# Loads moved to SyncE, and more turned attention blocks sent by way of device memory

## The chip, the cores and the metric

The kernel runs on one core of a Trainium2 chip. The metric is the device time of one execution in microseconds, median of several runs. The engines are named as in the profile: PE (TensorE), DVE (VectorE), ACT (ScalarE), POOL (GpSimd) and SP (SyncE, which here only issues DMAs).

## What is computed

An attention with a threshold, whose result is the input of an MLP:

```python
scores = scale * np.matmul(q, k.transpose(0, 1, 3, 2))        # q, k, v: (8, 8, 576, 64)
thresh = np.max(scores, axis=-1, keepdims=True) - tau
scores = np.where(scores >= thresh, scores, -1000000000.0)
scores = scores - np.max(scores, axis=-1, keepdims=True)
attn = np.exp(scores)
attn = attn / (np.sum(attn, axis=-1, keepdims=True) + 1e-09)
attn_out = np.matmul(attn, v)
x = attn_out.transpose(0, 2, 1, 3).reshape(4608, 512)
h = x @ w_in                                                   # (512, 2048)
r = np.maximum(h, 0.0)
out = (r * r) @ w_out                                          # (2048, 512)
```

Everything is float32.

## The kernel before

**Visits and steps.** The attention goes over pairs of heads. A *visit* is one pair of heads with its query blocks (four of 128 queries and one of the 64 left over), and a *step* `s` is one query block of a visit. The first eight visits (n=0 to 7) split the first four pairs in two; from n=8 on a visit is a whole pair. The step loop is written out by hand, and each engine executes its instructions in the order in which the program issues them.

In a step the score products go to PSUM on PE (`scores`, `scores_of_two`), DVE takes the maxima (`maxima`, L305), ACT the exponentials (`exponents`, L320), DVE applies the threshold and sums (`threshold`, L332 to L335), and POOL divides (`divide`, L340 and L342).

**Turning.** For the product with v, the weights `w` must be turned, so that keys lie on partitions, in the tile `wT`. Up to n=10 PE does it (`turn`). From n=11 on (`by_dma`) DVE turns blocks of 32 by 32 into one of two halves of the tile `turned` (`turn_blocks`, L427 to L437), and DMAs from SyncE put the blocks in their places in `wT` (`place_blocks`). Two query blocks of a visit share one half of `turned`, a *pair* of blocks: pair 0 is query blocks 0 and 1, pair 1 is blocks 2 and 3, and pair 2 holds the left-over block. There are two ways to place one:

- Direct: 16 DMAs of 72 KB from `turned` to `wT` (L453; for pair 2 they are L458 and L466).
- Through device memory: one DMA of 1152 KB writes the half to the device tensor `aside` (`set_aside`, L404), and four DMAs of 288 KB read it back into `wT` (L445). `turned` is free again after the first.

From n=12 on visits are *paired*: the left-over blocks of an even and an odd visit are treated as one step at the head of the even visit, so two visits take nine steps. Only pair 0 of odd visits goes through `aside` before the change; the function `aside_first` says so. Lists by step, filled at L955 to L990, say in which step a pair is placed (`place_at`), a load is asked for (`load_at`), and q or k is turned by DVE for use (`prep_at`).

**Mixing.** `mix` (L499) multiplies the turned weights by v some steps after the visit's last block: three steps for an odd visit, four for an even one. A step with a mix is called *valued* in the code. It reads `wT`, so a placing of the next blocks to the same rows has to wait for it.

**Loads.** From n=11 on, q, k, v and left-over rows are asked for some steps ahead and put in a queue `loads`. `some_loads` (L198), called four times in a step, takes one or two from it and issues them. Which engine issues them is decided in its last line: SyncE up to two steps after the first step of n=11 (`first_dma + 2`), GpSimd after that.

**The MLP.** As soon as 256 rows of x are complete, they are a *chunk*. Its products (`unit`, L658; `product`, L764) are cut into pieces that the function `fill` puts between the attention's instructions of each step, at a rate worked out in advance. The MLP uses sums of weight factors, made by GpSimd and in part by DVE (`factor_sum`, L589), and sums of tokens (L635).

**The order in a step.** Steps before n=12's first (`first_late`) are issued in the body of the last loop, later ones by `late_step`. In the body the blocks of n=11 are turned near the end of a step, after the threshold of the step (L1167). In `late_step` they are turned right behind the exponentials (`turn_last`).

Of the kernel before, what the change touches and what calls it, by code (L numbers as in the profile page):

```python
# [19 lines left out]
def kernel(  # L20
# [10 lines left out]
    nc = tc.nc  # L31
# [6 lines left out]
    NBLK = S // P  # L38
# [159 lines left out]
    def some_loads():  # L198
        for _ in range(min(1 + (len(loads) > 8), len(loads))):
            to, src = loads.popleft()  # L200
            (nc.gpsimd if state["step"] > first_dma + 2 else nc.sync).dma_start(out=to, in_=src)  # L201

    def arrived(t):
        assert all(x[0].tensor.name != t.tensor.name for x in loads)
# [109 lines left out]
    def exponents(vis, i):  # L314
        w, sc, st = weights[vis, i]
        mx, thr, bias = (st[:, j, 0:len(sc)] for j in range(3))
        nc.scalar.activation(out=bias, in_=mx, func=AF.Copy, scale=-SCALE)  # L317
        nc.scalar.activation(out=thr, in_=mx, func=AF.Identity, bias=ntau8)
        for u in range(len(sc)):
            nc.scalar.activation(out=w[:, u, :].rearrange("p (h k) -> p h k", h=2), in_=sc[u],  # L320
                                 func=AF.Exp, bias=bias[:, u:u + 1], scale=SCALE)
# [78 lines left out]
    def set_aside(vis, pair):  # L400

        t = aside[len(outside) % 4]
        at = list(blocks).index((vis, pair)) % 2 * NB
        nc.sync.dma_start(out=t, in_=turned[:, at:at + NB])  # L404
        outside[vis, pair] = t.rearrange("(b r) (j x) -> r j b x", r=32, j=4)
# [33 lines left out]
    def place_blocks(vis, pair, which=range(4)):  # L439

        wb = blocks[vis, pair]
        if (vis, pair) in outside:
            for j in range(4):
                g0 = (ONE, TWO)[pair] // REST
                nc.sync.dma_start(out=wT[j * 32:j * 32 + 32, g0:g0 + 4, :, :].rearrange("r b c q -> r b (c q)"),  # L445
                                  in_=outside[vis, pair][:, j, :, :])
            return
        for qb in which:
            rows = slice(qb * 32, qb * 32 + 32)
            for j in range(4):  # L450
                to = wT[j * 32:j * 32 + 32, :, :, :]
                if pair < NBLK // 2:
                    nc.sync.dma_start(out=to[:, (ONE, TWO)[pair] // REST + qb, :, :].rearrange("p c q -> p (c q)"),  # L453
                                      in_=wb[rows, :, j, :, :].rearrange("p c u q -> p (c u q)"))
                    continue
                at = slice(qb % 2 * 32, qb % 2 * 32 + 32)
                if paired(vis):
                    nc.sync.dma_start(out=to[:, (LEFT if qb < 2 else ODD) // REST, :, at], in_=wb[rows, j:2 * KB:4, :])  # L458
                else:


                    first = j if qb < 2 else KB + (j - KB) % 4
                    n = len(range(first, KB if qb < 2 else 2 * KB, 4))
                    c = first // 4
                    first += 2 if qb < 2 else -KB
                    nc.sync.dma_start(out=to[:, LEFT // REST, c:c + n, at], in_=wb[rows, first:first + 4 * n - 3:4, :])  # L466
# [151 lines left out]
    def some_later(engine):  # L618
        if later[engine]:
            make(*later[engine].popleft())  # L620
# [194 lines left out]
    def paired(n):  # L815

        return n >= 3 * HP
# [4 lines left out]
    steps = [(n, i) for n in range(len(visits)) for i in visits[n][1]]  # L822
    NST = len(steps)

    def by_dma(n):

        return n >= 3 * HP - 1

    first_dma = next(s for s in range(NST) if by_dma(steps[s][0]))
# [30 lines left out]
    state = {"us": 0.0, "left": 0.0, "step": 0, "free": False, "rounded": 0, "usable": 0, "then": [], "last": [], "made": 0}  # L860
# [76 lines left out]
    for s, (n, i) in enumerate(steps):  # L937
        if s < HP * FIRST:
            x = int(n > 0 and i == 0)
        else:  # L940
            x = 2 if (n, i) in ((2 * HP - 2, FIRST + 1), (2 * HP - 1, FIRST + 1), (2 * HP, FIRST)) else 1
# [14 lines left out]
    for s, (n, i) in enumerate(steps):  # L956
        if not by_dma(n) or i != visits[n][1][0] or paired(n) and n % 2:
            continue
        nxt = n + (2 if paired(n) else 1)
        more = nxt < len(visits)  # L960
        if paired(n):

            a, b = (1, 2) if paired(n - 1) else (2, 2)
            place_at[s + a].append((n, 2, (0, 1)))
            place_at[s + b].append((n, 2, (2, 3)))
            place_at[s + 3].append((n, 0))
            place_at[s + 5].append((n, 1))
            place_at[s + 8].append((n + 1, 0))
            place_at[s + 9].append((n + 1, 1))
            prep_at[s - 1].append(lambda n=n: prep_part(q, n))  # L970
            load_at[s - 1].append(lambda n=n: load_part(q, n + 1))
            load_at[s + 2].append(lambda n=n: load_v(n))
            prep_at[s + 3].append(lambda n=n: prep_part(q, n + 1))
            load_at[s + 4].append(lambda n=n: load_v(n + 1))
        else:
            place_at[s + 3].append((n, 0))
            place_at[s + 4].append((n, 1))
            place_at[s + 5].append((n, 2))
        if more:
            a, b, c, d = (s + 1, s + 5, s + 7, s + 8) if paired(n) else (s + 1, s + 2, s + 4, s + 4)  # L980
            load_at[a].append(lambda n=nxt: load_part(k, n))
            if paired(n):
                load_at[a].append(lambda n=nxt: load_left(n))
            prep_at[b].append(lambda n=nxt: prep_part(k, n))
            load_at[b].append(lambda n=nxt: load_part(k, n + 1))
            if not paired(n):
                load_at[s - 8].append(lambda n=nxt: load_left(n))
            load_at[b].append(lambda n=nxt: load_part(q, n))
            prep_at[c].append(prep_left)
            prep_at[d].append(lambda n=nxt: prep_part(k, n + 1))  # L990
# [16 lines left out]
    def turn_last(s):  # L1007
        if s <= NST:
            turn_blocks(*steps[s - 1])
            if aside_first(steps[s - 1][0]) and steps[s - 1][1] == 1:  # L1010
                set_aside(steps[s - 1][0], 0)

    def aside_first(n):

        return paired(n) and n % 2

    def at_least(count, made):
        while waiting and state["made"] < made + count:
# [2 lines left out]
    def late_step(s):  # L1021

        on = s < NST
        odd = on and steps[s][1] % 2 == 1
        if on:
            n, i = steps[s]
            if not odd:
                scores_of_two(s)
            after()
            maxima(s, [area(u, odd) for u in range(2)])  # L1030
            some_later("gpsimd")
            exponents(n, i)
        turn_last(s)
        valued = s in mixes and s < END

        def place():
            for what in place_at[s]:
                place_blocks(*what)

        if not valued:  # L1040
            place()

        def values():
            if s in mixes:
                while (visits[mixes[s][0]][0] // HP + 1) * S - RING > read_to["x"]:
                    piece()
                mix(*mixes[s])
                for j in chunk_at.get(s, ()):
                    add_chunk(j)

        if s == END:
            values()
        quarter = rate(s) / 4 if s < END else 1e9
        made = state["made"]
        fill(quarter)
        some_later("gpsimd")
        after()
        if on:
            threshold(n, i)
            for fn in prep_at[s] + load_at[s]:  # L1060
                fn()
            divide(n, i)
        some_later("vector")
        fill(quarter)
        after()
        some_later("gpsimd")
        if valued:
            at_least(1, made)
            made = state["made"]
            values()  # L1070
            place()
        some_loads()
        some_later("vector")
        some_loads()
        fill(quarter)
        some_loads()
        fill(quarter)
        some_loads()
        if valued:
            at_least(2, made)  # L1080

    for s in range(END + 1):
# [32 lines left out]
            turn(*old, 1)  # L1115
        if on:
            exponents(n, i)
            for p in now[1:]:
                round_weights(p, 0)
            if at == 1:  # L1120
                split_left(n)
            if lay:
                prep(n + 1)
            elif now:
                for p in now:
                    round_weights(p, 1)
# [36 lines left out]
        if smooth:  # L1163
            fill(quarter)
            after()
            some_later("gpsimd")
        if 0 < s <= NST and by_dma(steps[s - 1][0]):  # L1167
            m, x = steps[s - 1]
            turn_blocks(m, x)
        for what in place_at[s]:  # L1170
            place_blocks(*what)
        some_loads()
# [53 lines left out]
```

## Time and profile before

The time is 1391.8 us, median of 3 runs (1389.78 to 1392.49). The profiled execution has a span of 1391.4 us and a mean granted PE clock of 0.979.

| engine | busy us | share of the span | instructions |
|---|---|---|---|
| PE matmul | 1320.4 | 95% | 9112 |
| PE weight load | 1092.0 | 78% | 9112 |
| DVE | 940.3 | 68% | 2026 |
| ACT | 583.1 | 42% | 1357 |
| POOL | 987.8 | 71% | 1229 |

The chain of work that ended last lies on PE for 68% of the span and on POOL for 14%, with 6% on DVE. These are shares of one path through the program and not idle times: while the chain runs on POOL, PE may well be busy with work that came earlier.

The DMA issues that matter for the change, from issue to landing (median):

| issue | from | count | KB each | us |
|---|---|---|---|---|
| wT<-turned (direct) | SP | 608 | 72 | 2.1 |
| wT<-turned (pair 2) | SP | 192 | 36 | 2.0 |
| aside<-turned | SP | 12 | 1152 | 4.4 |
| wT<-aside | SP | 48 | 288 | 5.2 |
| ql<-in_q_dram | POOL | 96 | 72 | 3.1 |
| kl<-in_k_dram | POOL | 88 | 72 | 3.0 |
| vs<-in_v_dram | POOL | 48 and 48 | 128 and 32 | 3.2 and 2.3 |
| q_left<-in_q_dram | POOL | 88 | 8 | 2.0 |

How to read what follows: in the view of waits a line names the engine and line that waited, what released it, and then the time in total, how often and the longest. In a timeline a line has start, duration, engine, source line, operation and count, and in brackets the idle time before it with its releaser. `<-` reads "from". An instruction that only issues a DMA takes issue time on its engine; the transfer goes on by itself.

### The profile page before, as it was taken

How to read it: one execution, taken by the hardware profiler on the slowest of the kernel's cores; microseconds unless marked ns; L12 is line 12 of the kernel's file. 1: busy time of each engine (PE TensorE's matmuls, PEld its weight loads, DVE VectorE, ACT ScalarE, POOL GpSimd, SP SyncE). 2: the span in 40 equal slices, each digit the busy share in tenths (PEclk: the TensorE clock that was granted, in tenths of full speed). 3: DMA queues.
4: the chain of work that ended last, by engine and by line, in shares of the span. 5: the costliest groups of instructions: out<-in, count | busy, mean ns of one | idle time of the engine just before them, and what ended most of it. 6: DMA issues, size and time to landing. Idle time of an engine off the chain costs nothing.

```text
span 1391.4 us, 25676 instructions
## 1 busy us (share of the span) xinstructions
PE 1320.4 (95%) x9112; PEld 1092.0 (78%) x9112; DVE 940.3 (68%) x2026; ACT 583.1 (42%) x1357; POOL 987.8 (71%) x1229
## 2 busy tenths in 40 slices
PE   7899999979999899989999999999999899999998
PEld 5676567758887778778887879888887778889997
DVE  6877775867786777767777787777676757722231
ACT  4777664215353434435342435353524242512322
POOL 3679774778786959597878788879696856653451
PEclk8999999989999999999999999999999999999999
DMA  8755431434545454545435454545434443230000
GB/s 153 162 149 142 121 82 26 95 68 141 101 137 105 120 129 105 130 92 139 103 114 117 101 141 94 147 99 145 93 114 100 106 113 86 89 81 1 16 16 16
DMA packets 200976, 142.28 MB, mean 102 GB/s; under 512 B 157552, under 2 KB 161936, under 8 KB 199312
## 3 DMA queue, kind: packets, MB, share of 16 engines
q1 hardware_dynamic: 180256, 109.25, 32.7%
q0 software_dynamic: 18288, 31.11, 8.7%
q8 instruction: 72, 1.18, 0.4%
q10 hardware_dynamic: 2304, 0.29, 0.2%
q14 instruction: 56, 0.46, 0.1%
HBM read 64.75 MB, written 23.59 MB: 63 GB/s over the span
## 4 chain that ended last, share of the span: by engine, by line
PE 68%; POOL 14%; DVE 6%; issue 3%; ACT 3%; SPq 3%; DMA 2%; ACTq 0%; DVEq 0%; POOLq 0%
PE big L658 21%; PE big L764 21%; PE big L502 9%; PE big L284 6%; PE big L550 3%; PE big L268 3%; POOL w L342 3%; POOL g L589 2%; PE big L729 2%; SPq L453 2%; PE big L381 2%; DVE st L305 2%; DVE w L332 1%; POOL gsum L589 1%; POOL q_left L201 1%
## 5 line engine op out<-in xcount | busy, mean ns | idle before, releaser
L305 DVE TENSOR_REDUCE st<-big 128x1 f32<-128x576 f32 x288 | 204.4, 748 | 154.0 <-PE big L284 119.9
L342 POOL TENSOR_SCALAR w<-w,st 128x576 f32<-128x576 f32 x269 | 245.5, 922 | 23.7 <-DVE st L335 16.4
L764 PE MATMUL big<-wo,gsum 128*128 128x256 f32 x1088 | 245.1, 382 | 2.3 <-DVE gsum L784 2.3
L764 PEld LDWEIGHTS big<-wo,gsum 128*128 128x128 f32 x1088 | 204.9, 190 | 40.2 <-issue 9.5
L332 DVE SCALAR_TENSOR_TENSOR w<-big,st,w 128x576 f32<-128x576 f32 x269 | 207.0, 805 | 27.7 <-ACT w L320 27.6
L658 PE MATMUL big<-xT,w_in_sb 128*128 128x128 f32 x1536 | 188.1, 277 | 3.7 <-DVE osb L794 2.3
L658 PEld LDWEIGHTS big<-xT,w_in_sb 128*128 128x128 f32 x1536 | 180.7, 193 | 9.5 <-issue 3.8
L764 PE MATMUL big<-wo,g 128*128 128x256 f32 x816 | 186.6, 382 | 0.2
L502 PE MATMUL big<-wT,vs 128*64 128x128 f32 (+7 forms) x1700 | 171.8, 360 | 15.6 <-DMA wT<-turned 10.0
L320 ACT ACTIVATE w<-big,st 128x576 f32<-128x576 f32 x269 | 183.6, 733 | 0.0
L340 POOL TENSOR_SCALAR st<-st 128x2 f32<-128x2 f32 (+1 forms) x148 | 36.4, 246 | 197.6 <-DVE w L332 190.0
L764 PEld LDWEIGHTS big<-wo,g 128*128 128x128 f32 x816 | 151.2, 190 | 26.7 <-issue 7.5
L502 PEld LDWEIGHTS big<-wT,vs 128*64 128x64 f32 (+1 forms) x1700 | 97.7, 138 | 86.6 <-issue 34.0
L317 ACT ACTIVATE st<-st 128x2 f32<-128x2 f32 (+1 forms) x148 | 30.3, 205 | 293.9 <-DVE st L305 293.0
L670 DVE TENSOR_TENSOR g<-big,g 128x512 f32<-128x512 f32 x96 | 64.9, 676 | 99.5 <-PE big L658 94.0
L284 PE MATMUL big<-kT,qT 64*128 64x256 f32 (+3 forms) x768 | 110.6, 425 | 1.4 <-DVE w L332 1.4
L284 PEld LDWEIGHTS big<-kT,qT 64*128 64x128 f32 x768 | 86.7, 191 | 17.2 <-issue 9.0
L427 DVE STREAM_TRANSPOSE turned<-w 128x512 f32<-128x512 f32 x100 | 70.0, 700 | 32.4 <-POOL w L342 22.4
L540 POOL TENSOR_TENSOR gsum<-g 128x512 f32<-128x512 f32 x34 | 44.0, 1294 | 67.0 <-ACT g L667 63.5
L666 ACT ACTIVATE g<-g 128x512 f32<-128x512 f32 x96 | 60.3, 629 | 68.6 <-DVE g L670 68.6
L667 ACT ACTIVATE g<-g 128x512 f32<-128x512 f32 x128 | 80.7, 630 | 4.1
L658 PE MATMUL big<-t,g 128*128 128x128 f32 x512 | 67.2, 290 | 12.7 <-POOL g L589 10.8
(119 smaller groups left out, 2264.1 us busy)
## 6 DMA issues: line engine op xcount, KB each, us to landing
wT<-turned SPq DMA_DIRECT2D x608, 72.0 KB, 2.1
aside<-turned SPq DMA_DIRECT2D x12, 1152.0 KB, 4.4
wT<-aside SPq DMA_DIRECT2D x48, 288.0 KB, 5.2
wo<-in_moe_w_in_dram SPq DMA_DIRECT2D x16, 512.0 KB, 4.6
wo<-in_moe_w_out_dram SPq DMA_DIRECT2D x16, 512.0 KB, 3.7
out_dram<-osb POOLq DMA_DIRECT2D x32, 256.0 KB, 2.5
ql<-in_q_dram POOLq DMA_DIRECT2D x96, 72.0 KB, 3.1
wT<-turned SPq DMA_DIRECT2D x192, 36.0 KB, 2.0
```

The lines of the kernel that those rows point to most:

```text
L284: nc.tensor.matmul(big[to, at + x0:at + x1], lhsT, keys[u * D:(u + 1) * D, x0:x1], start=True, stop=True)
L305: nc.vector.tensor_reduce(out=mx[:, u:u + 1], in_=sc[u], axis=AX.XY, op=ALU.max)
L320: nc.scalar.activation(out=w[:, u, :].rearrange("p (h k) -> p h k", h=2), in_=sc[u], func=AF.Exp, bias=bias[:, u:u + 1], scale=SCALE)
L332: nc.vector.scalar_tensor_tensor(out=wu, in0=sc[u], scalar=thr[:, u:u + 1], in1=wu, op0=ALU.is_ge, op1=ALU.mult, accum_out=sm[:, u:u + 1])
L342: nc.gpsimd.tensor_scalar(out=w[:, u, :], in0=w[:, u, :], scalar1=z[:, u:u + 1], scalar2=rcp[:, u:u + 1], op0=ALU.add, op1=ALU.mult)
L427: move(wb[:, 0:h, :, :], whole_[:, 0, :, :, :])
L502: nc.tensor.matmul(ps[u * D:(u + 1) * D, :], vs[n % 2][rows, u * (NBLK + 1) + c, :], wT[rows, at // REST:(at + ps.shape[1]) // REST, NBLK ...
L658: nc.tensor.matmul(to[:, f, :], factor(j, p, q, c)[:, f * P:(f + 1) * P], part[:, c, :], start=(p in "125" and f == 0 and c == 0), stop=(p ...
L666: nc.scalar.activation(out=to, in_=to if src is None else src, func=AF.Relu)
L667: nc.scalar.activation(out=to, in_=to, func=AF.Square)
L670: nc.vector.tensor_tensor(out=x, in0=to, in1=x, op=ALU.add)
L764: nc.tensor.matmul(to, left[:, f, :], wo[:, slot, f, :], start=(f == 0), stop=(f == HF - 1))
```

## The change

There are three parts. All queued loads are issued by SyncE. Pair 0 and pair 1 of every visit from n=11 on go through `aside`, with the exception of pair 1 of odd paired visits, which is still placed directly; and a pair that goes out is placed later in its step, behind the first load. The blocks of n=11, the 12th visit, are turned behind the maxima and exponentials of the next step and no longer near its end, and its pair 0 is placed one step earlier. The purpose is to relieve GpSimd of issuing loads, to relieve SyncE of issuing sixteen DMAs for a pair, and to have the 12th visit's blocks ready sooner.

```diff
     def some_loads():
         for _ in range(min(1 + (len(loads) > 8), len(loads))):
             to, src = loads.popleft()
-            (nc.gpsimd if state["step"] > first_dma + 2 else nc.sync).dma_start(out=to, in_=src)
+            nc.sync.dma_start(out=to, in_=src)
...
-            place_at[s + 3].append((n, 0))
+            place_at[s + 2].append((n, 0))
             place_at[s + 4].append((n, 1))
             place_at[s + 5].append((n, 2))
...
     def turn_last(s):
         if s <= NST:
             turn_blocks(*steps[s - 1])
-            if aside_first(steps[s - 1][0]) and steps[s - 1][1] == 1:
-                set_aside(steps[s - 1][0], 0)
-
-    def aside_first(n):
-
-        return paired(n) and n % 2
+            n, i = steps[s - 1]
+            if i % 2 and by_dma(n) and goes_out(n, i // 2):
+                set_aside(n, i // 2)
+
+    def goes_out(n, pair):
+
+        return pair < NBLK // 2 and not (pair and paired(n) and n % 2)
...
         valued = s in mixes and s < END
 
-        def place():
-            for what in place_at[s]:
-                place_blocks(*what)
+        todo = list(place_at[s])
+
+        def place(all_):
+            for what in list(todo):
+                if all_ or not goes_out(*what[:2]):
+                    place_blocks(*what)
+                    todo.remove(what)
 
         if not valued:
-            place()
+            place(False)
...
             values()
-            place()
         some_loads()
+        place(True)
         some_later("vector")
...
         if on:
             exponents(n, i)
+            if s and by_dma(steps[s - 1][0]):
+                turn_last(s)
...
-        if 0 < s <= NST and by_dma(steps[s - 1][0]):
-            m, x = steps[s - 1]
-            turn_blocks(m, x)
         for what in place_at[s]:
             place_blocks(*what)
```

## The prediction

> **What bounds the kernel now.** I read the busy times first, then the stages, then the waits of TensorE, then GpSimd and SyncE where those waits fall. The stage view has, for each stretch, its length and each engine's busy time with its number of instructions, then the granted clock, DMA share and GB/s. The stretches are: all that lies before the 12th visit (n=11), that visit, the paired visits, the last chunks.
>
> ```profile
> 0.00:229.00 229.00, 205.49 (x1510) 143.09 (x1512) 163.10 (x361) 149.76 (x368) 158.50 (x189) 0.97 0.53 127
> 229.00:300.00 71.00, 61.02 (x339) 47.52 (x335) 48.23 (x98) 16.79 (x45) 50.96 (x60) 0.90 0.28 60
> 300.00:1216.00 916.00, 882.39 (x6134) 743.85 (x6133) 681.89 (x1502) 371.97 (x864) 708.04 (x917) 0.98 0.47 114
> 1216.00:1391.00 175.00, 171.48 (x1136) 157.59 (x1135) 47.04 (x67) 44.54 (x83) 70.25 (x64) 1.00 0.10 26
> ```
>
> TensorE (PE, first number after the length) is the bound everywhere, so only its idle time and its half-speed clock can be won. In the 12th visit it is idle 71.0 - 61.0 = 10.0 us; in the paired visits 916.0 - 882.4 = 33.6 us. The rest of its idle time lies before 229 us or after 1216 us, where the change touches nothing. Next, who ends those waits (us in total, times, longest):
>
> ```profile
> PE big L658 <- POOL g L589: 10.8, 8, 3.7
> PE big L658 <- POOL gsum L589: 10.1, 4, 3.8
> PE big L502 <- DMA wT<-turned: 10.0, 2, 6.2
> ```
>
> The third line is the whole idle time of the 12th visit: the value products of its mix (L502) wait for blocks that SyncE hasn't finished placing. The first two are 20.9 of the 33.6 us in the paired visits: products of the MLP wait for factor sums that GpSimd makes (L589). The other 12.7 us end on VectorE in pieces of about 1 us. Why GpSimd is late shows in its timeline ahead of the longest such wait:
>
> ```profile
> 597.78 2.69 POOL L201 DMA_DIRECT2D kl<-in_k_dram  x4
> 600.47 1.07 POOL L201 DMA_DIRECT2D q_left<-in_q_dram  x2
> 601.62 0.22 POOL L340 TENSOR_SCALAR st<-st 128x2 f32<-128x2 f32 x1
> 601.94 1.63 POOL L342 TENSOR_SCALAR w<-w,st 128x576 f32<-128x576 f32 x2
> 603.51 2.72 POOL L201 DMA_DIRECT2D q_left<-in_q_dram  x5
> ...
> 609.11 3.38 POOL L589 TENSOR_TENSOR g<-g,w_in_sb 128x512 f32<-128x512 f32 x2
> ```
>
> The reader is to see that 11 load issues (L201) of 2.69 + 1.07 + 2.72 = 6.48 us stand in GpSimd's queue between its last idle moment (591.5 us) and the sums that TensorE waits for. TensorE's own timeline has the price, in brackets:
>
> ```profile
> 610.88 0.49 PE L658 MATMUL big<-t,g 128*128 128x128 f32 x2 [3.69 <-POOL g L589]
> 612.55 6.50 PE L658 MATMUL big<-t,g 128*128 128x128 f32 x30 [1.18 <-POOL g L589]
> ```
>
> I went back from each of the larger GpSimd waits in this way: since GpSimd's last idle moment there were 3.4 to 12.0 us of L201, always more than the wait (2.65 us at 318, 1.13 at 384, 2.64 at 469, 1.03 at 544, 3.69 at 607, 2.00 at 1026, 3.81 at 1112).
>
> For the 12th visit, SyncE's timeline against TensorE's:
>
> ```profile
> 244.16 30.00 SPq L453 DMA_DIRECT2D wT<-turned  x32
> 274.26 10.40 SPq L466 DMA_DIRECT2D wT<-turned  x16
> ```
> ```profile
> 281.11 1.30 PE L502 MATMUL big<-wT,vs 128*64 128x320 f32 x2 [6.16 <-DMA wT<-turned]
> 286.23 7.08 PE L502 MATMUL big<-wT,vs 128*64 128x320 f32 x38 [3.83 <-DMA wT<-turned]
> ```
>
> SyncE needs 48 issues in a row; the second block pair is turned at 263 us, its 16 issues end at 274.3, the left-over ones at 284.7, and the mix, which TensorE reached at 275.0, is released near 286.
>
> [...] GpSimd pays in its own time: 368 issues of L201 occupy it for 66.9 + 64.6 + 59.1 + 48.2 = 238.8 us. [...] the trace has SyncE standing 50.6 us in 12 waits of the placing line L445 on `aside<-turned`. [...] the clock is 0.90 in the 12th visit and 0.97 or 0.98 exactly in the sub-stages with long waits, 1.00 at 800 to 1000 us, where there are nearly none.
>
> **The change part by part.**
>
> *Loads to SyncE.* GpSimd loses 238.8 us of 988 us. SyncE gains 184 q and k loads x 0.49 us (its rows at L179), 96 of v x 0.53 (L225), 88 of q_left x 0.43 (L196): 90 + 51 + 38 = 179 us.
>
> *Turned blocks through device memory.* By the program 38 block pairs are placed directly now (608 issues of 72 KB), 12 by way of `aside`. Afterwards 38 go out (2 per even visit, 1 per odd one, 2 of the 12th) and 12 stay direct. SyncE loses 26 x 16 = 416 issues x 0.589 = 245 us and gains 26 x 0.342 + 104 x 0.386 = 49 us. In sum SyncE's issue time goes 179 - 245 + 49 = -17 us: it has the room. Latency of a pair: direct 16 x 0.63 + 2.1 = 12 us; out and back 4.4 + 4 x 0.43 + 5.2 = 11.3 us, the same within 1 us, and even mixes have 10 us or more between the last placed packet and its use.
>
> *DMA engines.* 26 more writes of 1.18 MB as 128 packets of 9216 B at 359 ns make 1195 us of engine time, and loads as 128 B packets at 13.2 ns instead of packets of 4 KB at 246 ns cost some 590 us more; over 16 engines 112 us, so the share goes from 0.47 to about 0.59 in the paired visits. Hidden, as no transfer is bandwidth-bound.
>
> *Order on SyncE.* Placing a pair that goes out now waits for its `aside` (about 5 us) near the end of the step, and loads queue behind it. Steps take 8.6 us on average and a load is consumed 3 or 4 steps after it is queued, so I charge nothing for slips of 5 us. The sharp place is the direct pair of odd visits: its 16 issues end at 437.50 us, the last packet at 438.63, and the mix's second group reads it at 440.55; over the 12 odd mixes this slack is 1.4 to 6.7 us. The queue ahead of it (four issues after the even mix, four loads) is done about 4 us before its blocks are turned, so I charge 3 us in all for it.
>
> *12th visit turned behind the maxima.* The second pair is turned at about 256.5 instead of 263 us, as GpSimd's division (253.6) and the maxima (254.8) allow. Out at 256.9, landed at 261.5, four issues to 263.2. The 16 left-over issues then start at the turn of block 4 (265.2) and end at 275.5, landed at 277.5. TensorE arrives at 275.0: 2.5 us of wait remain of 10.0, saving 7.5.
>
> *Sum.* GpSimd's waits: 20.9 us, of which I take 85% (GpSimd also waits 190.0 us for the thresholds on VectorE, and part of its lead will end there): 18. The waits on VectorE, partly late through GpSimd (22.4 us of VectorE's turning waits are for its division): 4 of 12.7. Clock: the mean 0.979 over 1391 us means 29 us lost, of which 7 before 229 us and 7 in the 12th visit, so some 15 in the paired visits; 11 of these return with the waits. 12th visit: 7.5 + 2.5, since the mix in half clock took 7.08 us for 38 products where later mixes take 4.8 for 40. Together 18 + 4 + 11 + 10 = 43, less 3: **1391.8 - 40 = 1352 us**.
>
> **The rivals.**
>
> *Another wait takes over (A).* GpSimd gets ahead and then stands for VectorE's thresholds, so that its sums come hardly earlier. For it: those 190.0 us of waits, in 61 pieces. Against it: in each case above there was more load time than wait in one unbroken run of work. If half of the paired visits' gain goes: 1391.8 - 10 - 16 = 1366 us.
>
> *Loads weren't what mattered (B).* Only the 12th visit gains: 1391.8 - 10 = 1382 us. For it: GpSimd is busy only 71% of the span. Against it: the same unbroken runs.
>
> *SyncE becomes the bound (C).* One queue in order carries loads, write-outs, and placings with waits. If each odd mix, with as little as 1.4 us of slack, waits 5 us and drags 1.7 us of half clock behind it, that is 12 x 6.7 = 80 us against 40 won: 1432 us; at 4 us each, 1400 us. For it: SyncE then issues about 47 us and waits some 20 us in each 77 us of two visits. Against it: its issue time falls, and the direct pairs, the sharp ones, are still taken early in the step.
>
> **How the numbers follow.** Chances: forecast 0.60 (1338 to 1360), A 0.17, B 0.09, C 0.14, with 0.02 of C's ending within 0.2% of before. So faster 0.86, same 0.02, slower 0.12. The range is 1337 to 1386 us: the low end is all 33.6 us, 12 us of clock and 9 us of the visit; the high end takes in A and B and leaves C out.
>
> **What would show it.** L201 appears only under SyncE; GpSimd falls to about 750 us busy; the two L658 lines on GpSimd lose most of 20.9 us; the clock of the paired visits is 0.99 or 1.00; the mix of the 12th visit waits under 4 us. Wrong, if L502 shows waits on `wT<-turned` or `wT<-aside` at odd mixes, if VectorE's turning of q or k waits for loads, or if waits of L658 on GpSimd stay while L340's waits for VectorE grow by what the loads took.

## The result, and the profile after

The changed kernel takes 1367.0 us (median of 4 runs, 1365.4 to 1368.6) against 1392.1 us before: a ratio of 0.982 with a 95% interval of 0.980 to 0.984. That is 25 us less. The forecast was 40 us less, 1352 us, with a range of 1337 to 1386 us. Of all the runs below one was slow, at a lower granted clock (0.94, 1382.4 us, of the version with pair 0 placed directly), and is left out.

The stage view after, in the same stretches of time as before (length, busy PE, PEld, DVE, ACT, POOL with their counts, clock, DMA share, GB/s):

```profile
0.00:229.00 229.00, 205.40 (x1508) 142.97 (x1510) 163.23 (x362) 149.43 (x367) 158.16 (x189) 0.97 0.53 127
229.00:300.00 71.00, 66.30 (x392) 53.81 (x388) 55.01 (x120) 20.93 (x54) 44.31 (x46) 1.00 0.51 111
300.00:1216.00 916.00, 891.79 (x6245) 754.18 (x6244) 672.27 (x1492) 370.99 (x863) 500.58 (x579) 0.99 0.64 146
```

The first stretch is unchanged. In the second, TensorE's idle time went from 10.0 to 4.7 us and its clock from 0.90 to 1.00. In the third it went from 33.6 to 24.2 us (the stretch now holds some later work too), while GpSimd's busy time fell by 207 us and the DMA share rose from 0.47 to 0.64. Over the whole page GpSimd is busy 757.8 us instead of 987.8.

TensorE's waits after (total, times, longest):

```profile
PE big L658 <- POOL gsum L589: 14.0, 3, 5.5
...
PE big L658 <- ACT g L678: 4.4, 1, 4.4
...
PE big L502 <- DMA wT<-turned: 3.6, 1, 3.6
```

Eight waits on `g` of L589 are gone. But three waits on `gsum` of L589 are left and have become longer: 14.0 us in three instead of 10.1 us in four. The 4.4 us on ScalarE (L678) are a new wait, at 601 us: ScalarE stands there behind exponentials that wait 5.01 us for VectorE's maxima (L317 on L305). It is in the trace of every version below with the loads on SyncE and in none with the loads on GpSimd. This is the longest wait on `gsum`:

```profile
313.63 3.35 PE L658 MATMUL big<-xT,gsum 128*128 128x128 f32 x14 [5.52 <-POOL gsum L589]
```

GpSimd's own waits say what holds it now. Before:

```profile
POOL st L340 <- DVE w L332: 190.0, 61, 11.3
...
POOL osb L635 <- DMA out_dram<-osb: 1.0, 2, 0.5
```

After:

```profile
POOL st L340 <- DVE w L332: 344.5, 88, 11.5
...
POOL osb L635 <- DMA out_dram<-osb: 17.4, 9, 5.1
```

The first line is large and grew by 154.5 us: GpSimd waits for VectorE's thresholds when it has nothing else to do. The second is small, and the experiments below show that it is the one that matters. GpSimd's timeline ahead of that longest wait, of the changed kernel:

```profile
304.23 0.62 POOL L742 DMA_DIRECT2D out_dram<-osb  x1
304.87 1.30 POOL L589 TENSOR_TENSOR gsum<-w_in_sb,g 128x512 f32<-128x512 f32 x1
311.04 0.72 POOL L635 TENSOR_TENSOR osb<-xT,t 128x256 f32<-128x256 f32 x1 [4.87 <-DMA out_dram<-osb]
311.71 0.57 POOL L742 DMA_DIRECT2D out_dram<-osb  x1
312.30 1.27 POOL L589 TENSOR_TENSOR gsum<-w_in_sb,g 128x512 f32<-128x512 f32 x1
```

The token sum called T4 (L635) writes its result over rows of `osb` that GpSimd has just sent to the output (a *write-out*, L742). It must stand until that transfer has landed, and the factor sum behind it, the one TensorE waits for, stands with it. The same place in the kernel before:

```profile
313.47 0.61 POOL L742 DMA_DIRECT2D out_dram<-osb  x1
314.11 1.30 POOL L589 TENSOR_TENSOR gsum<-w_in_sb,g 128x512 f32<-128x512 f32 x1
315.33 2.15 POOL L201 DMA_DIRECT2D vs<-in_v_dram  x3
317.47 0.76 POOL L635 TENSOR_TENSOR osb<-xT,t 128x256 f32<-128x256 f32 x1
```

There the write-out landed 2.6 us after its issue, under three load issues that GpSimd had to make anyway. After the change the loads are gone from this place, and the write-out took 6.75 us. SyncE's timeline in that moment shows why it might:

```profile
301.66 1.73 SPq L445 DMA_DIRECT2D wT<-aside  x4
303.44 5.87 SPq L201 DMA_DIRECT2D vs<-in_v_dram  x7
```

Four reads of 288 KB and seven loads of v had just been issued on SyncE's queue. From the DMA packets in the trace: the first packet of this write-out began 4.77 us after its issue (1.16 us where nothing collides), and until it landed SyncE's queue kept the 16 engines busy for 100% of the time, with 331 packets of 2304 B and 2064 of 256 B. Averaged over the 33 write-outs that GpSimd issues, the landing went from 2.88 to 3.57 us, and those over 3.5 us from 5 to 12.

### The profile page after: what moved, and what is told of

The parts are those of the page before. It is cut to its first block, busy times and chain, and to the rows that moved or that the text cites. A ratio compares the mean times of both kernels' runs of the same rounds, so it can differ in the third digit from the quotient of the medians.

```text
span 1363.7 us, 25169 instructions
## 1 busy us (share of the span) xinstructions
PE 1307.4 (96%) x9112; PEld 1085.8 (80%) x9112; DVE 929.3 (68%) x2026; ACT 583.1 (43%) x1357; POOL 757.8 (56%) x861
## 3 DMA queue, kind: packets, MB, share of 16 engines
q1 hardware_dynamic: 327232, 162.07, 52.4%
q10 hardware_dynamic: 2304, 0.29, 0.2%
## 4 chain that ended last, share of the span: by engine, by line
PE 84%; DVE 4%; POOL 4%; ACT 3%; DMA 2%; issue 2%; SPq 1%; ACTq 0%; DVEq 0%; POOLq 0%
PE big L764 28%; PE big L658 26%; PE big L502 11%; PE big L284 8%; PE big L550 3%; PE big L268 3%; PE big L729 2%; PE big L381 2%; DVE st L305 1%; DVE w L332 1%; DMA out_dram<-osb 1%; ACT wT L382 1%; ACT w L320 1%; POOL w L342 1%; POOL g L589 1%
## 5 line engine op out<-in xcount | busy, mean ns | idle before, releaser
L305 DVE TENSOR_REDUCE st<-big 128x1 f32<-128x576 f32 x288 | 204.5, 749 | 151.9 <-PE big L284 116.8
L340 POOL TENSOR_SCALAR st<-st 128x2 f32<-128x2 f32 (+1 forms) x148 | 36.8, 248 | 349.8 <-DVE w L332 344.5
L658 PE MATMUL big<-xT,w_in_sb 128*128 128x128 f32 x1536 | 187.3, 277 | 2.2 <-DVE osb L794 2.1
L658 PEld LDWEIGHTS big<-xT,w_in_sb 128*128 128x128 f32 x1536 | 180.1, 193 | 7.5 <-issue 4.0
L502 PE MATMUL big<-wT,vs 128*64 128x128 f32 (+7 forms) x1700 | 168.8, 356 | 9.1 <-ACT wT L382 4.0
L502 PEld LDWEIGHTS big<-wT,vs 128*64 128x64 f32 (+1 forms) x1700 | 96.4, 136 | 78.4 <-issue 26.5
L317 ACT ACTIVATE st<-st 128x2 f32<-128x2 f32 (+1 forms) x148 | 30.3, 205 | 273.0 <-DVE st L305 272.0
L284 PE MATMUL big<-kT,qT 64*128 64x256 f32 (+3 forms) x768 | 107.8, 419 | 0.0
L658 PE MATMUL big<-xT,gsum 128*128 128x128 f32 x512 | 68.8, 290 | 14.5 <-POOL gsum L589 14.0
```

What stands on the lines that cost most here:

```text
L284: nc.tensor.matmul(big[to, at + x0:at + x1], lhsT, keys[u * D:(u + 1) * D, x0:x1], start=True, stop=True)
L305: nc.vector.tensor_reduce(out=mx[:, u:u + 1], in_=sc[u], axis=AX.XY, op=ALU.max)
L502: nc.tensor.matmul(ps[u * D:(u + 1) * D, :], vs[n % 2][rows, u * (NBLK + 1) + c, :], wT[rows, at // REST:(at + ps.shape[1]) // REST, NBLK ...
L658: nc.tensor.matmul(to[:, f, :], factor(j, p, q, c)[:, f * P:(f + 1) * P], part[:, c, :], start=(p in "125" and f == 0 and c == 0), stop=(p ...
```

## The experiments

Each is timed against runs of the kernel before on the same chip. Those took 1391.9 to 1393.2 us from chip to chip, so a difference between versions of different chips is good to about 1 us. Theory M in the expectations is: the extra waits come from write-outs that land late. The numbers below are medians of 4 runs, with pair 0 placed directly of 3, with more pairs through device memory alone of 12.

**Loads alone.** The kernel before with the one line:

```diff
-            (nc.gpsimd if state["step"] > first_dma + 2 else nc.sync).dma_start(out=to, in_=src)
+            nc.sync.dma_start(out=to, in_=src)
```

> The kernel before, with the loads issued by SyncE and nothing else changed. Theory M (what is left of the waits after the change comes from write-outs of osb that land late because the DMA engines are fuller): 1372 to 1378 us, most of the gain of the paired visits, with the 12th visit unchanged at about 10 us of TensorE idle time; write-outs issued by GpSimd land in 2.9 us on average as before (3.6 after the change), so GpSimd's token sum L635 waits under 6 us in all for them (17.4 after the change). Rival R (SyncE hasn't the room for loads as long as each pair costs 16 issues): 1385 us or more, with waits of L502 on wT<-turned at the odd mixes or of VectorE on loads.

Measured: 1362.6 us, ratio 0.979 (0.977 to 0.980). One part of the change alone gains 30.5 us, more than the whole change, and the time is 9 us below M's range. TensorE's waits:

```profile
PE big L502 <- DMA wT<-turned: 13.9, 5, 7.2
...
PE big L658 <- POOL gsum L589: 3.3, 3, 1.6
```

The waits on GpSimd are 3.3 us instead of 20.9. Of the 13.9 us, 10.95 are the 12th visit's; the other 2.95 are new, at odd mixes (1.44 us the longest), whose direct pairs come later when loads share SyncE. Write-outs land in 3.06 us on average, and L635 waits 6.8 us for them, both a little over what M allowed. So SyncE has room for the loads with sixteen issues a pair, nearly.

**Loads back.** The changed kernel with that line undone.

> The changed kernel with its loads back on GpSimd as before (aside and the earlier turning of the 12th visit stay). Theory M: 1380 to 1384 us; TensorE's waits of L658 on GpSimd are back at about 20 us, and only the gain of the 12th visit (about 10 us) is left. Rival R (the blocks through device memory make the gain): 1370 us or less.

Measured: 1385.1 us, ratio 0.995 (0.9935 to 0.9965), 1 us above M's range. TensorE's waits on GpSimd are back, L635 waits 2.5 us for write-outs, and the 12th visit's gain is what is left:

```profile
PE big L658 <- POOL gsum L589: 11.3, 4, 3.8
PE big L658 <- POOL g L589: 10.0, 8, 3.7
...
PE big L502 <- DMA wT<-turned: 3.4, 1, 3.4
```

**The 12th visit alone.** The kernel before with its blocks turned behind the exponentials; all pairs are placed by sixteen direct issues.

```diff
-            place_at[s + 3].append((n, 0))
+            place_at[s + 2].append((n, 0))
...
             exponents(n, i)
+            if s and by_dma(steps[s - 1][0]):
+                turn_last(s)
...
-        if 0 < s <= NST and by_dma(steps[s - 1][0]):
-            m, x = steps[s - 1]
-            turn_blocks(m, x)
```

> The kernel before, with the blocks of the 12th visit turned behind the maxima and its pair 0 placed a step earlier, all placed directly by 16 issues. Theory M: the second pair is turned some 6.5 us earlier, so SyncE's chain of 48 issues ends some 6.5 us earlier: 1383 to 1386 us, the wait of L502 on wT<-turned near 3.5 us. Rival R (the way through aside is needed for that): 1389 us or more, a wait over 7 us.

Measured: 1383.0 us, ratio 0.994 (0.992 to 0.995), 10.2 us less than before. The wait of L502 on `wT<-turned` is 2.6 us, shorter than the 3.6 us after the whole change. The way through device memory isn't needed for this gain.

**More pairs through device memory, alone.** The kernel before with pairs 0 and 1 of even paired visits going out as well.

> The kernel before with pairs 0 and 1 of even paired visits going through aside as well, loads on GpSimd, the 12th visit as before. Theory M: load issues stand between a write-out and the token sum on GpSimd and hide its landing, so nothing is lost or won by more than 4 us: 1389 to 1396 us. Rival R (the transfers cost by themselves): 1397 us or more.

Measured: 1391.4 us, ratio 0.999 (0.9985 to 1.0002): nothing. The write-outs do land late here, 12 of 33 over 3.5 us, as many as in the changed kernel. But T4 hardly waits for them:

```profile
POOL osb L635 <- DMA out_dram<-osb: 2.0, 4, 1.0
```

So with the loads on GpSimd late write-outs are covered by its load issues, as M says.

**Loads and the 12th visit, without more pairs going out.** The changed kernel with:

```diff
     def goes_out(n, pair):
-        return pair < NBLK // 2 and not (pair and paired(n) and n % 2)
+        return paired(n) and n % 2 and pair == 0
```

> The changed kernel with only pair 0 of odd paired visits going through aside, as before the change: loads on SyncE and the earlier turning stay. Theory M (sending more pairs through device memory costs time, since it makes write-outs land late under GpSimd's token sum): the gains of loads alone and of the 12th visit alone add up, 30.5 + 10.2 us, so 1351 to 1355 us, and L635 waits under 8 us for write-outs. Rival R (the pairs through device memory are needed to give SyncE room for the loads): 1365 us or more.

Measured: 1351.2 us, ratio 0.971 (0.969 to 0.972). The two gains add up (30.5 + 10.2 = 40.7; measured 40.8). So sending more pairs through device memory, which alone costs nothing, costs 1367.0 - 1351.2 = 16 us once the loads are on SyncE. (The new place behind the first load of the step stays in this version, so it costs nothing that shows in the sum.) Both waits are short again:

```profile
POOL osb L635 <- DMA out_dram<-osb: 5.7, 8, 1.2
...
PE big L658 <- POOL gsum L589: 3.0, 3, 1.2
```

**The token sum later.** The changed kernel with T4 asked for at product 6, so that it comes behind the factor sums on GpSimd:

```diff
             if p == "1":
...
                 nc.scalar.copy(g11, to)
-                ask((j, "T4"))
...
             elif p == "6":
                 nc.scalar.copy(g12, to)
+                ask((j, "T4"))
```

> The changed kernel with the token sum T4, which GpSimd writes over osb rows that are being written out, asked for at product 6 instead of product 1, behind a factor sum that TensorE waits for. Theory M: GpSimd no longer stands for the write-out there, L635's 17.4 us of waits fall below 6, TensorE's 14.0 us on gsum L589 below 5, and with the half-clock stretches behind them 1356 to 1361 us. Rival R (GpSimd is held by VectorE's thresholds anyway, L340 waits 344.5 us): 1365 to 1369 us, with the same waits of TensorE under another releaser.

Measured: 1348.7 us, ratio 0.969 (0.967 to 0.970), 18.3 us less than the changed kernel and more than expected. GpSimd's timeline at the same place:

```profile
308.26 0.62 POOL L742 DMA_DIRECT2D out_dram<-osb  x1
308.91 1.29 POOL L589 TENSOR_TENSOR gsum<-w_in_sb,g 128x512 f32<-128x512 f32 x1
310.13 0.57 POOL L742 DMA_DIRECT2D out_dram<-osb  x1
310.73 1.28 POOL L589 TENSOR_TENSOR gsum<-w_in_sb,g 128x512 f32<-128x512 f32 x1
...
315.58 0.74 POOL L635 TENSOR_TENSOR osb<-xT,t 128x256 f32<-128x256 f32 x1
```

The write-out still lands late here (6.7 us at this place, 3.82 us on average), but T4 has no wait for write-outs left. Of the waits for them only 4.7 us remain in all, at sums that GpSimd writes to the other rows of `osb`. TensorE has no wait on `gsum` left in its list, and its stretches at half clock (granted clock 0.50) after 250 us, the one at the very end apart, sum to 6.8 us instead of 20.5. In the trace of the changed kernel there are four of these, and each begins 3.3 to 4.4 us after TensorE fell idle for a wait of 3.46 to 5.52 us; three of the waits are those on `gsum`, the fourth is the one on ScalarE. GpSimd still waits 339.4 us for thresholds, which shows that those waits weren't what delayed the sums.

**The token sum later, on the version without more pairs going out.**

> The same with the token sum T4 asked for at product 6. Theory M: with the token sum out of the way both ways of placing cost about the same, so 1345 to 1351 us, within 4 us of the changed kernel with T4 later (1348.7). Rival R (the extra transfers slow something else as well): below 1343 us.

Measured: 1348.2 us, ratio 0.969 (0.967 to 0.970): level with the one above. Without the additional pairs, moving T4 gains 3 us (1351.2 to 1348.2); with them it gains 18 us. With T4 out of the way the additional transfers cost nothing that can be measured, so their 16 us are the cost of T4's waits for write-outs and of what follows from these.

**The token sum later, in the kernel before.**

> The kernel before with the token sum T4 asked for at product 6 and nothing else changed. Theory M (its place matters only once the loads don't stand ahead of it and hide the write-out): gain of at most 6 us, 1386 to 1393 us. Rival R (GpSimd's order at this place costs in any case, so the gain of 18 us has nothing to do with the change): 1380 us or less.

Measured: 1384.8 us, ratio 0.995 (0.993 to 0.997): 7.3 us, just over what M allowed and far from the 18.3 us. T4's place costs something in any case, as it stands ahead of a sum that TensorE needs (TensorE's waits on `gsum` go from 10.1 to 7.3 us); the larger part of its cost came with the change. Since moving T4 gains only 3 us where the additional pairs are left out, it came with these.

**Which transfers collide.** In the changed kernel one of the two pairs of even visits is placed directly again.

```diff
# e9_pair0_direct
-        return pair < NBLK // 2 and not (pair and paired(n) and n % 2)
+        return pair < NBLK // 2 and not (paired(n) and pair != (n % 2 == 0))
# e10_pair1_direct
-        return pair < NBLK // 2 and not (pair and paired(n) and n % 2)
+        return pair < NBLK // 2 and not (pair and paired(n))
```

> The changed kernel with pair 0 of even paired visits placed directly, pair 1 still through aside. Theory M (write-outs collide with the read-back of pair 0, which SyncE issues in the step in which a chunk's write-outs start): write-outs at chunk ends land in about 3 us, and of the 16 us between the changed kernel (1367.0) and the one without more pairs through aside (1351.2) most is back: 1352 to 1358 us. Rival R (any additional transfer counts, by the total load on the DMA engines): about half is back, 1358 to 1362 us.

> The changed kernel with pair 1 of even paired visits placed directly, pair 0 still through aside. Theory M: 1362 to 1368 us, TensorE's waits on gsum L589 stay above 9 us. Rival R: about half is back, 1357 to 1361 us.

Measured: 1353.8 us with pair 0 direct, ratio 0.972 (0.970 to 0.974), and 1360.9 us with pair 1 direct, ratio 0.977 (0.976 to 0.979), so 13 and 6 of the 16 us come back. The first is in M's range. The second is 1 us below M's range and at the edge of R's, though TensorE's waits on `gsum` stay at 10.0 us, as M said. What speaks against R is that the DMA share of the paired visits is nearly the same in both, 0.59 and 0.58 (0.64 in the changed kernel), while the gains are 13 and 6 us. The landing of single write-outs tells more than the sums. Worked out from the packets and the semaphores in the traces, us from issue to landing, by the place in the program:

```
write-out near (us)      304    454   1006   1078   1152
changed kernel          6.75   5.54   4.53   6.95   4.28
pair 0 direct           2.48   2.71   4.31   5.21   2.98
pair 1 direct           6.80   5.84   2.83   2.53   4.66
loads and 12th visit    2.44   2.91   2.85   2.88   2.55
```

The write-outs near 304, 454 and 1152 us run into the read-back of pair 0, those near 1006 and 1078 us into that of pair 1. These five follow the burst they fall into and not the total load on the DMA engines. Not every late write-out comes from the additional pairs: one takes 6.36 us near 872 us in the changed kernel, and 6.46 us without these pairs. And a read-back is not the whole burst, since loads stand right behind it, near 304 us seven of v. With pair 0 direct these go out later too, from 310.95 us instead of 303.44, so this experiment takes both away from the write-out near 304 us.

**The v loads later.** The changed kernel with `load_v(n)` of even visits asked for at `s + 4` instead of `s + 2`.

> The changed kernel with the v loads of even paired visits asked for two steps later, so that they don't stand right behind the read-back of pair 0. Theory M1 (read-back and v loads together fill the engines for some 7 us under the write-out): 1353 to 1361 us. Theory M2 (the read-back alone does it): 1364 to 1369 us.

Measured: 1364.9 us, ratio 0.980 (0.979 to 0.982), M2's number. It settles little: the loads queued next moved up into the gap, and the write-out near 304 us still had 1280 packets of 256 B beside it. Whether the read-back or the loads behind it weigh more stays open.

## Why the prediction was right, and where it was off

The direction and the mechanism of the gain were right, and the time lies in the stated range. The size of the gain was too large by 15 us: 1367.0 us is outside 1338 to 1360, to which the prediction gave 0.60, and 1 us from rival A's number. One term of the sum accounts for that. One of the signs failed with it: the two L658 lines on GpSimd were to lose most of 20.9 us, and 14.0 us were left.

- *12th visit, 10 us:* measured alone 10.2 us. The turned blocks, issues and landing came within about 2 us of the times worked out; the wait that was to remain at 2.5 us is 3.6 us after the change.
- *GpSimd without the load issues, 18 + 4 + 11 us less 3 for the odd mixes, so 30:* measured alone 30.5 us. That it fits so closely is in part luck: in the profiled execution of the loads alone TensorE's idle time is 15 us less, where the terms say 19, and its busy time, which holds the half-clock stretches, is 15.5 us less, where they say 11. The new wait of 4.4 us on ScalarE was in no term. The small loss at odd mixes exists where pairs are placed directly (2.95 us) and not after the change.
- *Turned blocks through device memory, costed at nothing:* this is the step that failed. It said of the additional transfers "Hidden, as no transfer is bandwidth-bound", from a mean DMA share of about 0.59. The mean came out at 0.64, but right behind a read-back the share was 1.10 (304 to 309 us) and 1.03 (1078 to 1084 us; packets that overlap are each counted), and one short transfer that something waits for, the write-out of `osb`, fell into such stretches. It cost 16 us: 11 us more of TensorE's waits on `gsum` (14.0 against 3.0 without those transfers) and, by the mean clock (0.987 of 1364 us against 0.991 of 1349 us, so 17.7 against 12.1 us lost), 5 to 6 us of clock. The prediction went through who waits for `wT` and for loads, but not through who waits for write-outs; in the trace before, that wait was 1.0 us, since load issues on GpSimd covered it. With the loads taken away alone it is 6.8 us, with the additional transfers alone 2.0 us, with both 17.4 us.
- *SyncE's issue time, 17 us less:* this sum was wrong too. SyncE's DMA issues take 702.0 us after the change and 646.5 before, 55.5 us more. The loads that moved take 243 us instead of 179: the median issue is 0.50 us for q and k, 0.61 us for v and 0.43 us for left-over rows, where 0.49, 0.53 and 0.43 were costed, but some take up to 2.8 us, and the mean is 0.66 us (0.54 us without the additional pairs). None of TensorE's waits is for a load.
- *Rival A, another wait takes over, at 1366 us,* had nearly the measured number for another reason: it named VectorE's thresholds. Those waits did grow by 154.5 us, and the sign given at the end of the prediction (waits of L658 on GpSimd stay while L340's grow) could have been taken for a proof. With T4 later, L340 still waits 339.4 us and the kernel gains 18.3 us. So A's mechanism falls, and that its number was nearly met is luck. Another wait did take over in part, but it was T4's for write-outs.
- *Rival B,* only the 12th visit gains: excluded. The loads alone gain 30.5 us, and with the loads back the time is 1385.1 us.
- *Rival C,* SyncE as the bound: not seen. The slack of the odd mixes is 1.7 to 6.3 us after the change (1.4 to 6.7 before), and no odd mix waits. A small form of it is visible in the loads alone, at 2.95 us.

The forecast of 1352 us is, in effect, the time of the version without the additional pairs (1351.2 us). The best versions found are that one with T4 later (1348.2 us) and the changed kernel with T4 later (1348.7 us), which can't be told apart.

## What to carry to other kernels

When instructions are taken off an engine's queue, look at what they were covering: a wait that shows as 1 us may be short only because the engine was busy until it ended (T4's for write-outs was 1.0 us before and 17.4 us after). A mean DMA share does not tell when a short transfer with a waiter lands (at a mean of 0.64 the write-outs landed in 2.0 to 7.0 us); for each one, ask which burst is in flight when it is issued. And before a multi-part change is kept whole, each part should be measured alone and beside the others, since here the part that was free alone cost 16 us beside another.

## What the runs showed of the hardware that was not expected

- A write-out issued from GpSimd is on another queue than SyncE's transfers (in the trace of the changed kernel q0, with 2,800 packets, and q1, with 327,232), and yet it can start late. For nine of the 12 late write-outs of the changed kernel, SyncE's packets kept the 16 engines busy for 94% or more of the time from the issue to the write-out's first packet, and that packet came 2.4 to 4.8 us after the issue, behind 18 to 133 of SyncE's packets per engine. Where no packet of SyncE's ran in that time, the first packet of a write-out of the same size came after 1.13 to 1.16 us. Full engines alone do not decide it: near 1086 us SyncE's packets took 93% of that time, and the write-out's first packet came after 1.13 us. What decides stays open.
- The same loads are cut differently by issuer. From GpSimd most of their bytes moved in packets of 4096 B (6656 of that size on its queue before, 2176 after, which are the write-outs' own), from SyncE in packets of 128 B and 256 B (131,008 before, 273,344 after). In the trace before, a packet of 4096 B took 246 ns on GpSimd's queue, and one of 128 B 13.2 ns on SyncE's, which makes 422 ns for 4096 B. In the version with loads alone the DMA share of the paired visits is 0.53 instead of 0.47. In the changed kernel the loads of v landed later (median 5.6 us for the larger ones, 3.2 before), and VectorE's waits for q did not grow (7.2 us, 7.6 before). In the trace before, loads of q and k landed in 2.5 to 2.6 us from SyncE and in 3.0 to 3.1 us from GpSimd. These times hold issue, queue and transfer together, and so do not show that the transfer time is the same.
